# Reordering the start of a fused attention and FFN kernel: the last v tile's copy, the kv matmuls and the small copies of the prologue

## The chip, the cores and the metric

The kernel runs on one core of a Trainium2 chip. The metric is device time in microseconds (us), the median of several executions; lower is better. The kernel before takes 211.5 us, and its executions spread over 0.4 us in the first rounds.

The engines are named as in the profile: PE (TensorE), PEld (its weight loads), DVE (VectorE), ACT (ScalarE), POOL (GpSimd) and SP (SyncE, which issues most of the DMA transfers here). "Line L262" is a line of the kernel's source.

## The reference, cut to what matters

```python
batch, n_heads, seq, head_dim, r = 4, 4, 1088, 32, 8
def phi(x):                                   # S1, S2 are [8, 32]
    a = einsum('rd,bhsd->bhsr', S1, x)
    b = einsum('rd,bhsd->bhsr', S2, x)
    return outer(a, b) flattened to 64 features
q_p, k_p = phi(q), phi(k)
kv  = einsum('bhsf,bhsd->bhfd', k_p, v)       # sum over the sequence
z   = sum of k_p over the sequence
out = (q_p @ kv) / (q_p . z + 1e-6)           # num / den
x   = out as [4352, 128]
return square(relu(x @ w_in)) @ w_out         # w_in [128, 2048], w_out [2048, 128]
```

The attention of a batch needs all of its k and v before its first output. So the first batch has a prologue, in which TensorE waits for other engines again and again. After it, the FFN of one chunk of rows runs beside the attention of the next.

## The kernel before: the parts that matter

The transfers of the first batch, in order. SyncE issues them, except part 2 of v (the last v tile), which ScalarE issues. A transfer is said here to land when the last of its 16 semaphore increments shows in the trace:

```python
load_qk(kn[0], k, 0, 0, 512)
load_qk(kn[0], k, 0, 512, S)
load_qk(qn[0], q, 0, 0, 384)          # first 384 columns of q
load_v(vn[0], 0, 0)
load_v(vn[0], 0, 2, (nc.scalar, nc.scalar))   # the last v tile, issued by ScalarE
load_v(vn[0], 0, 1)
# ... w_in: two transfers of 512 KB
load_qk(qn[0], q, 0, 384, S)          # the other columns of q
# ... w_o: two transfers of 512 KB
```

GpSimd's small copies, which stand ahead of its copy of the last v tile:

```python
for h in range(H):
    for j_, o_, f_ in (...three patterns...):
        nc.gpsimd.tensor_copy(_ap(sr, ...), _ap(s_T, ...))     # 12 copies
for h in range(H):
    nc.gpsimd.tensor_copy(sq[...], s_T[:, 0:16])               # 4 copies
iden = cpool.tile([128, 128], F32); make_identity(nc, iden[:])
iden16 = ...; nc.gpsimd.tensor_copy(iden16[:], iden[:])
```

And the order of the prologue, which is each engine's order too, since the schedule is by hand:

```python
keep_warm(WARM0)                      # 11 matmuls on zeros
# ... kf (features of k), fs (their copy), four groups of tiles: 2, 2, 4, 1
replicated(2, 0, 128, psf, "pg")
a_v(0, 0, nc.scalar); a_kp(0, 0); a_kv0(0); a_kp(0, 1)
a_kv(0, 0); a_kv(0, 1)                # kvp += v_t^T kp_t
replicated(0, 0, 128, psa, "feat"); replicated(1, 0, 128, psa, "tr")
a_fs(0, 2); a_fs(0, 3)
a_v(0, 1, nc.scalar)
a_v(0, 2, nc.gpsimd)                  # the last v tile, 64 rows
a_kp(0, 2); a_kp(0, 3)
for t in range(2, 9): a_kv(0, t)
nc.scalar.copy(qb[:, 0:128], rep[2, 0][:, 0:128]); products(0, 128)
# ... replicated(j, 128, 384) for j = 2, 0, 1
nc.scalar.copy(qb[:, 128:384], rep[2, 128][:, 0:256])
a_kvz(0)                              # kvp transposed and copied: 8 small copies
products(128, 384)
# ... w_in cast to 16 bits on ScalarE
for t in range(3): a_nd(0, t)         # numerators and denominators
a_qT(0, 384, S)                       # VectorE transposes the other columns of q
a_qc(0, 1); a_qc(0, 2, psf, "po")     # TensorE, from that transpose
keep_warm(WARM)                       # 4 more matmuls on zeros
a_x1(0, 0); a_x2(0, 0)                # den, rden, mx, ... on VectorE
a_x3(...); a_xp(...); a_xT(...)       # xs, its transpose xp, the FFN's input xT
```

The names: kvp is the sum of v times features of k, and kvz its transposed copy; rep is S applied to q, from which `products` forms q's features qp; nd holds numerators and denominators; qc is S applied to the other columns of q, for later chunks; pg is the first product of the FFN. The warm matmuls compute nothing: they hold TensorE's clock up.

## Time and profile before

| | before |
|---|---|
| median | 211.5 us (211.44 to 211.83, 4 runs) |
| profiled execution | span 209.2 us |
| last v tile copied | 11.37 to 11.65 us |
| last kvp matmul ends | 12.12 us |
| nd ends | 15.28 us |
| den starts | 15.32 us |
| first FFN matmul, pg | 18.15 us |

The table by windows shows where TensorE is full (columns: window, its length, busy time and instructions of PE, PEld, DVE, ACT, POOL, then TensorE's clock, DMA share, GB/s).

```profile
10.00:15.00 5.00, 4.12 (x58) 3.39 (x54) 2.96 (x10) 2.14 (x5) 1.77 (x8) 1.00 1.04 341
...
25.00:40.00 15.00, 15.00 (x97) 9.16 (x97) 12.02 (x35) 12.92 (x28) 6.15 (x32) 1.00 0.03 10
```

From 25 us on PE is busy all of the time. Nothing that the change does touches that part, so its worth is how much earlier the FFN starts.

The chain of waits of the first 21 us, in order of time (start, duration, what):

```profile
...
6.87 1.59 POOL sr L228 x3
8.51 1.13 POOL sq L233
...
11.42 0.24 POOL va_119 L253
...
11.70 0.42 PE kvp L321 x8
12.12 1.49 PE rep L598 x6
...
13.69 1.60 PE nd L382 x12
```

GpSimd works through sr, sq and the identity and only then copies the last v tile. The last eight kvp passes wait for that copy, and rep and nd follow on TensorE with hardly a gap.

The timeline of the same stretch (start, duration, engine, line, operation; in brackets the idle time before and what ended it):

```profile
11.37 0.28 POOL L253 COPY va_119<-vn 64x128 f32<-64x128 f32 x1
11.70 0.42 PE L321 MATMUL kvp<-kp,va_119 128*33 128x64 f32 x8 [0.80 <-POOL va_119 L253]
13.69 1.59 PE L382 MATMUL nd<-kvz_125,qp 128*128 128x132 f32 x12
14.07 0.90 DVE L259 STREAM_TRANSPOSE qT<-qn 128x704 f32<-128x704 f32 x1
15.32 0.17 DVE L398 TENSOR_SCALAR den<-nd 128x12 f32<-128x12 f32 x1 [0.34 <-PE nd L382]
18.15 0.22 PE L477 MATMUL pg<-xT,w_in 128*128 128x128 f16 x1
```

The transpose of q's other columns starts at 14.07 us, and the semaphore events of the trace show the transfer that it reads (qn, columns 384 on) landing at 14.01 us.

### The profile page before, as it was taken

The page shows a single profiled execution, that of the slowest core. Times are in us where ns is not written, and L with a number is a line of the kernel's source. Part 1 is how long each engine was busy: PE and PEld are TensorE (multiplying, and loading weights), DVE is VectorE, ACT ScalarE, POOL GpSimd, SP SyncE. Part 2 cuts the span into 40 slices and gives each one's busy share as a digit, 9 for nine tenths or more (in the row PEclk, how much of TensorE's full clock was granted, in tenths as well). Part 3 has the DMA queues.
Part 4 walks back from the last instruction along what each step waited for, and adds up shares of the span by engine and source line. Part 5 has one row for each costly group of instructions (what it writes and reads, how often), then busy time and mean ns, then how long its engine had stood idle before and what let it go on. Part 6 is the DMA issues. An engine that isn't in the chain of part 4 may idle for free.

```text
span 209.2 us, 3744 instructions
## 1 busy us (share of the span) xinstructions
PE 200.6 (96%) x1213; PEld 125.3 (60%) x1213; DVE 146.5 (70%) x393; ACT 145.1 (69%) x327; POOL 61.9 (30%) x254
## 2 busy tenths in 40 slices
PE   7988999999999999999999999999999999999980
PEld 2864675566677655567676655557766655555650
DVE  3856967948597697795577877695487776667740
ACT  2555988747898876487888776487887775756740
POOL 4924556010076840010573700010573500000001
PEclk9999999999999999999999999999999999999998
DMA  6599400200047220020006710020002010110201
GB/s 186 144 342 245 132 0 3 36 5 0 0 75 190 96 33 0 3 39 0 2 12 165 185 31 0 3 39 3 0 6 33 0 31 3 19 19 0 38 0 32
DMA packets 26728, 11.24 MB, mean 54 GB/s; under 512 B 18822, under 2 KB 25286, under 8 KB 26710
## 3 DMA queue, kind: packets, MB, share of 16 engines
q1 hardware_dynamic: 26244, 10.89, 21.4%
q8 instruction: 9, 0.15, 0.3%
q10 hardware_dynamic: 386, 0.07, 0.2%
q0 software_dynamic: 80, 0.07, 0.1%
q14 instruction: 9, 0.07, 0.1%
HBM read 8.78 MB, written 2.23 MB: 53 GB/s over the span
## 4 chain that ended last, share of the span: by engine, by line
PE 68%; issue 20%; POOL 5%; DVE 3%; DMA 1%; POOLq 0%; ACT 0%; ACTq 0%; DVEq 0%
PE po L499 39%; PE pg L477 11%; PE nd L382 8%; PE kvp L321 4%; PE qc L356 3%; POOL br L515 2%; PE kf L275 2%; POOL sr L228 1%; DMA s_nat<-in_S_dram 1%; PE xp L455 1%; POOL sq L233 1%; PE rep L598 1%; DVE xs L439 1%; DVE mx L403 0%; POOLq L786 0%
## 5 line engine op out<-in xcount | busy, mean ns | idle before, releaser
L486 ACT ACTIVATE gt<-pg 128x384 f32<-128x384 f32 (+2 forms) x193 | 89.5, 465 | 42.6 <-PE pg L477 41.0
L477 PE MATMUL pg<-xT,w_in 128*128 128x384 f16 (+2 forms) x193 | 61.1, 317 | 0.5 <-ACT xT L464 0.3
L515 POOL COPY br<-beta 32x3 f32<-32x3 f32 x192 | 44.3, 231 | 55.7 <-DVE beta L446 48.3
L477 PEld LDWEIGHTS <-w_in 128*128 128x128 f16 x193 | 18.8, 98 | 18.9 <-issue 1.7
L568 POOL DMA_DIRECT2D out_dram<-obl x1 | 0.8, 813 | 38.6 <-DVE obl L559 38.6
L366 DVE STREAM_SHUFFLE qa<-qc 128x384 f32<-128x384 f32 x22 | 11.9, 592 | 0.0
L382 PEld LDWEIGHTS nd<-kvz_127,qp 128*128 128x128 f32 x72 | 10.0, 190 | 2.5
L382 PEld LDWEIGHTS nd<-kvz_125,qp 128*128 128x128 f32 x72 | 9.7, 190 | 2.9 <-issue 0.4
L301 DVE TENSOR_TENSOR kp<-fs 128x1024 f32<-128x1024 f32 (+3 forms) x10 | 11.0, 1110 | 0.5 <-ACT fs L289 0.2
L371 DVE TENSOR_TENSOR qp<-qa,qb 128x384 f32<-128x384 f32 x22 | 11.2, 548 | 0.1
L382 PE MATMUL nd<-kvz_127,qp 128*128 128x132 f32 x72 | 10.1, 276 | 0.0
L382 PE MATMUL nd<-kvz_125,qp 128*128 128x132 f32 x72 | 10.0, 277 | 0.1
L398 DVE TENSOR_SCALAR den<-nd 128x12 f32<-128x12 f32 x12 | 2.0, 171 | 11.3 <-PE nd L382 11.3
L523 DVE STREAM_TRANSPOSE oT<-po 128x384 f32<-128x384 f32 (+1 forms) x11 | 6.2, 564 | 5.4 <-PE po L499 5.2
L342 POOL COPY kvz_127<-kvt 32x2 f32<-32x2 f32 x8 | 1.5, 185 | 28.3 <-DVE kvt L332 28.0
L356 PE MATMUL qc<-qT,sq 128*128 128x384 f32 x22 | 9.0, 496 | 0.0
L464 ACT COPY xT<-xp 128x384 f16<-128x384 f16 (+3 forms) x13 | 5.6, 428 | 2.3 <-PE xp L455 2.2
L581 PE MATMUL warm<-zero 128*128 128x512 f16 x15 | 5.8, 557 | 1.2 <-DVE zero L142 1.2
L439 DVE TENSOR_TENSOR xs<-nd,sc 128x384 f16<-128x384 f32 (+2 forms) x13 | 6.7, 520 | 0.2
L321 PEld LDWEIGHTS kvp<-kp,va_122 128*33 128x33 f32 x144 | 4.3, 111 | 3.8 <-issue 3.8
L361 DVE STREAM_SHUFFLE qb<-qc 128x384 f32<-128x384 f32 x11 | 6.5, 590 | 0.0
L321 PEld LDWEIGHTS kvp<-kp,va_119 128*33 128x33 f32 x144 | 4.3, 111 | 3.4 <-issue 2.2
(677 smaller groups left out, 431.1 us busy)
## 6 DMA issues: line engine op xcount, KB each, us to landing
vn<-in_v_dram SPq DMA_DIRECT2D x32, 64.0 KB, 3.7
kn<-in_k_dram SPq DMA_DIRECT2D x3, 544.0 KB, 4.8
qn<-in_q_dram SPq DMA_DIRECT2D x3, 544.0 KB, 3.4
out_dram<-ob SPq DMA_DIRECT2D x32, 48.0 KB, 1.8
w_in_99<-in_moe_w_in_dram SPq DMA_DIRECT2D x2, 512.0 KB, 4.7
w_o<-in_moe_w_out_dram SPq DMA_DIRECT2D x2, 512.0 KB, 9.4
out_dram<-ob SPq DMA_DIRECT2D x12, 40.0 KB, 1.7
qn<-in_q_dram SPq DMA_DIRECT2D x1, 352.0 KB
```

What stands on the lines that cost most here:

```text
L301: nc.vector.tensor_tensor(out=_ap(kp, 0, 128, 0, [[64, 4 * n], [8, 8], [1, 8]]), in0=_ap(fs, 0, 128, 0, [[8, 4 * n], [1, 8], [0, 8]]), in1 ...
L321: nc.tensor.matmul(kvp[c : c + 33, 64 * (h // 2) : 64 * (h // 2) + 64], va[b % 2][:, 132 * t + 33 * h : 132 * t + 33 * h + 33], kp[:, c0 + ...
L356: nc.tensor.matmul(qc[:, 0:384], sq[:, :], qT[:, 384 * ch : 384 * ch + 384])
L361: nc.vector.stream_shuffle(in_=st[b, "qc", ch][:, 0:384], out=qb[:, :], mask=mask_b)
L366: nc.vector.stream_shuffle(in_=st[b, "qc", ch][:, 0:384], out=qa[:, :], mask=mask_a[e])
L371: nc.vector.tensor_tensor(out=qp[:, :], in0=st[b, "qa", ch, e][:, :], in1=st[b, "qb", ch][:, :], op=mult)
L382: nc.tensor.matmul(nd[:, 132 * o : 132 * o + 132], st[b, "qp", ch, e][:, 128 * o : 128 * o + 128], st[b, "kvz"][:, 132 * e : 132 * e + 132 ...
L439: nc.vector.tensor_tensor(out=_ap(st[b, "xs", ch], 0, 128, 128 * o, [[32, 4 * n], [1, 32]]), in0=_ap(st[b, "nd", ch], 0, 128, 132 * o, [[3 ...
L477: nc.tensor.matmul(pg[:, c0:c1], w_in[:, 128 * c : 128 * c + 128], st[b, "xT"][:, 384 * ch + c0 : 384 * ch + c1],)
L486: nc.scalar.activation(gt[:, c0:c1], pg[:, c0:c1], Relu)
L499: nc.tensor.matmul(st["po", b, ch][:, c0:c1], w_o[:, 128 * c : 128 * c + 128], g2s[i][1][:, c0:c1], start=(c == 0 and c0 == 0), stop=(c == ...
L515: nc.gpsimd.tensor_copy(_ap(st[b, "br"], 32 * dm, 32, 12 * ch + p0, [[4, 3]]), st[b, "beta"][32 * p0 : 32 * p0 + 32, 3 * ch : 3 * ch + 3],)
```

## The change

The intent is to end the kvp sums sooner. The last v tile is copied ahead of sq and the identity; four of the twelve sr copies go to ScalarE; four kv tiles instead of two run ahead of the replicated features; kp is grouped 2, 2, 2, 3; the v copy is split; the eight kvz copies, already shared by VectorE, ScalarE and GpSimd, are shared out differently and stand ahead of the second qb copy; and there are two warm matmuls less. (A short description that came with it says that ScalarE copies the last v tile. The diff leaves that copy on GpSimd, earlier in its order.)

```diff
-    WARM0, WARM = 11, 4
+    WARM0, WARM = 10, 3
-    KG = [[(0, 2), (2, 2), (4, 4), (8, 1)]] + ...
+    KG = [[(0, 2), (2, 2), (4, 2), (6, 3)]] + ...
+    a_kv0(0)                       # moved up from behind a_kp(0, 0)
-    for h in range(H):
-        for j_, o_, f_ in (... three patterns, all nc.gpsimd ...):
+    for j_, o_, f_, copy in (
+        (2, ..., nc.gpsimd.tensor_copy),
+        (1, ..., nc.scalar.copy),
+        (0, ..., nc.gpsimd.tensor_copy),
+    ):
+        for h in range(H):
-    # sq copies and the identity stood here
     (in a_kvz)
-            block(nc.vector, h)
+            block(nc.vector if b > 0 or h < 2 else nc.scalar, h)
-            ones(nc.gpsimd if b > 0 or h < 2 else nc.scalar, h)
+            ones(nc.gpsimd if b > 0 or h > 1 else nc.vector, h)
     (in the prologue)
-    a_kv(0, 0)
-    a_kv(0, 1)
+    for t in range(4):
+        a_kv(0, t)
-    a_v(0, 1, nc.scalar)
     a_v(0, 2, nc.gpsimd)
+    # sq copies and the identity, now here
+    a_v(0, 1, nc.scalar, 0, 2)
     a_kp(0, 2)
+    a_v(0, 1, nc.scalar, 2, 2)
     a_kp(0, 3)
-    for t in range(2, 9):
+    for t in range(4, 9):
+    a_kvz(0)
     nc.scalar.copy(qb[:, 128:384], rep[2, 128][:, 0:256])
-    a_kvz(0)
```

More of the change, by code (lines that the diff above doesn't have):

```diff
@@ L79 @@
     E = 2
-    WARM0, WARM = 11, 4
+    WARM0, WARM = 10, 3
     LA = 3
-    KG = [[(0, 2), (2, 2), (4, 4), (8, 1)]] + [[(0, 4), (4, 5)]] * (B - 1)
+    KG = [[(0, 2), (2, 2), (4, 2), (6, 3)]] + [[(0, 4), (4, 5)]] * (B - 1)
     add = mybir.AluOpType.add
@@ L197, with a_kv0 @@
     st = {}
+    def a_kv0(b):
+        st[b, "kvp"] = psa.tile([128, 512], F32, tag="acc", bufs=2, name="kvp")
+        nc.vector.memset(st[b, "kvp"][:, 0:128], 0.0)
+    a_kv0(0)
     def a_kT(b, part):
@@ L225 @@
         )
-    for h in range(H):
-        for j_, o_, f_ in ((2, 8, [[0, 4], [1, 8]]), (0, 0, [[1, 4], [0, 8]]), (1, 4, [[1, 4], [0, 8]])):
-            nc.gpsimd.tensor_copy(
+    for j_, o_, f_, copy in (
+        (2, 8, [[0, 4], [1, 8]], nc.gpsimd.tensor_copy),
+        (1, 4, [[1, 4], [0, 8]], nc.scalar.copy),
+        (0, 0, [[1, 4], [0, 8]], nc.gpsimd.tensor_copy),
+    ):
+        for h in range(H):
+            copy(
                 _ap(sr, 32 * h, 32, 128 * j_ + 32 * h, [[8, 4], [1, 8]]),
@@ L231, with a_v @@
             )
-    for h in range(H):
-        nc.gpsimd.tensor_copy(
-            sq[32 * h : 32 * h + 32, 32 * h : 32 * h + 16], s_T[:, 0:16]
-        )
-    iden = cpool.tile([128, 128], F32)
-    make_identity(nc, iden[:])
-    iden16 = cpool.tile([128, 128], F16)
-    nc.gpsimd.tensor_copy(iden16[:], iden[:])
     mask_b = [8 + l % 8 for l in range(32)]
     mask_a = [[4 * e + l // 8 for l in range(32)] for e in range(E)]
-    def a_v(b, part, eng):
+    def a_v(b, part, eng, t0=0, n=4):
         a = va[b % 2]
@@ L248, in a_v @@
             copy(
-                _ap(a, 0, 128, 528 * part, [[33, H], [132, 4], [1, 32]]),
-                _ap(vn[b], 0, 128, 512 * part, [[128, H], [32, 4], [1, 32]]),
+                _ap(a, 0, 128, 528 * part + 132 * t0, [[33, H], [132, n], [1, 32]]),
+                _ap(vn[b], 0, 128, 512 * part + 32 * t0, [[128, H], [32, n], [1, 32]]),
             )
@@ L308, in a_kp @@
             st[b, "kp", t0 + i] = kp, 256 * i
-    def a_kv0(b):
-        st[b, "kvp"] = psa.tile([128, 512], F32, tag="acc", bufs=2, name="kvp")
-        nc.vector.memset(st[b, "kvp"][:, 0:128], 0.0)
     def a_kv(b, t):
@@ L614 @@
     a_kp(0, 0)
-    a_kv0(0)
     a_kp(0, 1)
-    a_kv(0, 0)
-    a_kv(0, 1)
+    for t in range(4):
+        a_kv(0, t)
     replicated(0, 0, 128, psa, "feat")
@@ L622 @@
     a_fs(0, 3)
-    a_v(0, 1, nc.scalar)
     a_v(0, 2, nc.gpsimd)
+    for h in range(H):
+        nc.gpsimd.tensor_copy(
+            sq[32 * h : 32 * h + 32, 32 * h : 32 * h + 16], s_T[:, 0:16]
+        )
+    iden = cpool.tile([128, 128], F32)
+    make_identity(nc, iden[:])
+    iden16 = cpool.tile([128, 128], F16)
+    nc.gpsimd.tensor_copy(iden16[:], iden[:])
+    a_v(0, 1, nc.scalar, 0, 2)
     a_kp(0, 2)
+    a_v(0, 1, nc.scalar, 2, 2)
     a_kp(0, 3)
-    for t in range(2, 9):
+    for t in range(4, 9):
         a_kv(0, t)
```

## The prediction

> **What bounds it now.** From about 20 us on, TensorE is the limit: the table by windows shows it 100% busy in every window from 25 to 200 us, and the chain of waits is almost only its matmuls. The change touches only the first 19 us; after them the order of instructions on each engine is the same. So the gain is how much earlier the first FFN matmul (pg, 18.15 us in the timeline) starts.
>
> Up to 15.3 us the chain of waits runs over GpSimd: twelve sr copies (5.24 to 8.46), four sq copies (to 10.44), the identity (to 11.4), the copy of the last v tile (to 11.66). Then come kvp's last 8 passes (11.70), rep 128:384 (12.12 to 13.61), nd (13.69 to 15.29), the DVE chain den to xs (15.32 to 17.85), xp, xT, pg.
>
> **What the change does.** (The short description says ScalarE copies the last v tile. The diff leaves it on GpSimd, ahead of sq and the identity.)
> - GpSimd: four of twelve sr copies (0.27 us each) go to ScalarE, which idles 3.07 us there. The last v tile is copied at about 7.4 instead of 11.4 us.
> - TensorE: one warm matmul less (0.43 us) lets kf start about 0.4 us earlier.
> - kp regrouped 2,2,2,3, the kvp memset (0.17 us) moved to idle time. ScalarE's first v copy stays at 7.38 because its DMA lands at 7.32, the second at 8.95 because its DMA lands at 8.85. The last kp still ends near 9.9.
> - So kvp ends at about 10.7 instead of 12.12: 1.4 us won. rep follows to about 12.2. kvz copies (0.2 us each) are shared and done before that. nd then ends at about 13.75 instead of 15.29.
>
> **Why most of it will not arrive.** den stands on VectorE behind the transpose of qT 384:1088 (0.90 us). The Trainium skill ("TensorE: Matmul & The Clock Gate", opening table) says VectorE's queue is strict FIFO. That transpose needs the qn transfer of columns 384 on, whose semaphore increments in the trace end at 14.01 us; the transpose started at 14.07. The transfers are issued by SyncE in the same order with the same waits, and none waits for compute, so that landing stays. Before, the landing and the end of the products (14.16) coincided, and it cost nothing. After, VectorE idles from about 12.8 to 14.05, transposes until 14.95, and den starts at about 14.98 instead of 15.32. Gain: 0.35 of the 1.5 us. qc also waits for this transpose, as before (15.03); three warm matmuls instead of four clear TensorE by about 17.2, when the first xs is ready.
>
> Other transfers do not bind: w_in lands at 11.7 and 13.0, w_o's first half at 16.8 (needed at 19.1).
>
> **Predicted:** 211.5 - 0.35 = 211.15 us, range 210.3 to 211.6. The chance of over 2% faster is 0.01, within 2% 0.985, slower by over 2% 0.005.
>
> **What the profile would show.** kvp's last matmuls end at 10.4 to 11.0 with no wait for GpSimd; nd ends by 14.0; VectorE's longest prologue wait is now qT <- DMA qn, 1 us or more, at about 14.0; den starts at 14.8 to 15.1 right behind qT, with no wait for nd; pg starts at about 17.8; the windows after 25 us are unchanged but shifted.
>
> **What would make it wrong.** If the qn transfer lands earlier in undisturbed runs than in this trace, up to 1.5 us shows (210.0). If it lands later, or TensorE's 1.3 us gap before qc lowers its clock, nothing or a small loss shows. If ScalarE's four sr copies are slower than 0.25 us and delay the first fs copy past 6.4, the kp chain slips, but 1.2 us of slack now covers that.

## The result, and the profile after

Ratios here and below are the mean time of one kernel's runs over that of the other's runs of the same rounds, so they are not quite the ratio of the medians.

| | before | after |
|---|---|---|
| median | 211.5 us | 210.64 us (210.21 to 211.34, 4 runs) |
| ratio | | 0.9959 (95%: 0.993 to 0.9988) |
| span of the profiled execution | 209.2 us | 208.4 us |
| last v tile copied | 11.37 to 11.65 | 8.58 to 9.48 |
| last kvp matmul ends | 12.12 | 10.73 |
| nd ends | 15.28 | 13.86 |
| qn (columns 384 on) lands | 14.01 | 13.61 |
| den starts | 15.32 | 14.47 |
| pg starts | 18.15 | 17.43 |

The kernel became 0.4% faster. The timeline after, the lines that answer to those of before:

```profile
8.58 0.90 POOL L256 COPY va_119<-vn 64x128 f32<-64x128 f32 x1
9.41 1.31 PE L319 MATMUL kvp<-kp,va_119 128*33 128x64 f32 x40
12.10 1.76 PE L380 MATMUL nd<-kvz_125,qp 128*128 128x132 f32 x12
13.63 0.91 DVE L262 STREAM_TRANSPOSE qT<-qn 128x704 f32<-128x704 f32 x1 [0.77 <-DMA qn<-in_q_dram]
14.47 0.13 DVE L396 TENSOR_SCALAR den<-nd 128x12 f32<-128x12 f32 x1
14.60 1.56 PE L354 MATMUL qc<-qT,sq 128*128 128x384 f32 x4 [0.74 <-DVE den L396]
17.43 0.90 PE L475 MATMUL pg<-xT,w_in 128*128 128x128 f16 x3
```

TensorE no longer waits for GpSimd in kvp, and nd ends 1.42 us sooner. But the transpose is now preceded by a wait of 0.77 us for the transfer, and den comes straight behind the transpose with no wait for nd in its brackets: only 0.85 us of the 1.42 reach den. The rest waits for q. qc, on TensorE, is put down to den, but the instruction that it needs is the transpose; the two end within 0.06 us of each other.

The chain of waits after, over the same 21 us, has no GpSimd in it any more:

```profile
2.14 3.91 DMA vn<-in_v_dram
...
7.86 5.75 DMA qn<-in_q_dram
...
13.63 0.91 DVE qT L262
14.54 0.07 DVE den L396
14.61 1.55 PE qc L354 x4
16.16 0.66 PE warm L579 x3
...
16.86 0.23 PE xp L453
```

The chain goes from the transfers of the first microseconds through SyncE's issues to the qn transfer, the transpose, qc, the warm matmuls and xp. So two paths lead from the transpose to the FFN: den to xs on VectorE, and qc and the warm matmuls on TensorE. The second is the longer one here by a little: xp's first weights (xs) are loaded at 16.67 us, but the warm matmuls hold TensorE until 16.82. Of den's 0.85 us, 0.72 reach pg. The full part is unchanged; the window from 25 to 40 us after:

```profile
25.00:40.00 15.00, 15.00 (x96) 8.76 (x96) 12.04 (x32) 13.00 (x29) 6.15 (x32) 1.00 0.06 15
```

### The profile page after: what moved, and what is told of

The parts are those of the page before. It is cut to its first block, busy times and chain, and to the rows that moved or that the text cites. A ratio compares the mean times of both kernels' runs of the same rounds, so it can differ in the third digit from the quotient of the medians.

```text
span 208.4 us, 3741 instructions
## 1 busy us (share of the span) xinstructions
PE 200.1 (96%) x1211; PEld 124.9 (60%) x1211; DVE 146.4 (70%) x393; ACT 146.2 (70%) x332; POOL 61.2 (29%) x250
## 4 chain that ended last, share of the span: by engine, by line
PE 68%; issue 19%; DMA 5%; POOL 2%; DVE 2%; SPq 1%; ACT 0%; POOLq 0%
PE po L497 39%; PE pg L475 11%; PE nd L380 7%; PE qc L354 4%; PE kvp L319 4%; DMA qn<-in_q_dram 3%; POOL br L513 2%; DMA vn<-in_v_dram 2%; PE kf L278 2%; PE xp L453 1%; SPq L103 1%; DVE qT L262 0%; SPq L158 0%; POOLq L792 0%; SPq L113 0%
## 5 line engine op out<-in xcount | busy, mean ns | idle before, releaser
L304 DVE TENSOR_TENSOR kp<-fs 128x512 f32<-128x512 f32 (+3 forms) x10 | 10.9, 1111 | 0.2
L319 PEld LDWEIGHTS kvp<-kp,va_122 128*33 128x33 f32 x144 | 4.3, 111 | 3.8 <-issue 3.8
L579 PE MATMUL warm<-zero 128*128 128x512 f16 x13 | 5.1, 557 | 1.2 <-DVE zero L142 1.2
L401 DVE TENSOR_REDUCE mx<-nd 128x12 f32<-128x384 f32 x12 | 5.9, 495 | 0.0
```

The lines of the kernel that those rows point to most:

```text
L304: nc.vector.tensor_tensor(out=_ap(kp, 0, 128, 0, [[64, 4 * n], [8, 8], [1, 8]]), in0=_ap(fs, 0, 128, 0, [[8, 4 * n], [1, 8], [0, 8]]), in1 ...
L319: nc.tensor.matmul(kvp[c : c + 33, 64 * (h // 2) : 64 * (h // 2) + 64], va[b % 2][:, 132 * t + 33 * h : 132 * t + 33 * h + 33], kp[:, c0 + ...
```

## The experiments

Theory A: after the change, the start of the FFN is set by the landing of the qn transfer, since den stands behind the transpose of q in VectorE's order. Rivals: the gain comes from kf starting 0.5 us sooner (one warm matmul less) and the shared copies, with nothing waiting for the transfer; or the change itself moved the landing.

All times that follow in one table; "before" was run in the same rounds.

| run | median us | before us | ratio (95%) |
|---|---|---|---|
| after_again | 210.80 | 211.40 | 0.9973 (0.9955 to 0.9990) |
| after_qn_early | 210.47 | 211.40 | 0.9961 (0.9942 to 0.9980) |
| before_qn_early | 211.20 | 211.40 | 0.9999 (0.9975 to 1.0024) |
| before_v_early | 210.92 | 211.40 | 0.9981 (0.9963 to 0.9999) |
| after_v_late | 211.39 | 211.48 | 0.9990 (0.9969 to 1.0010) |
| after_qn_late | 217.76 | 211.48 | 1.0303 (1.0266 to 1.0339) |
| after_warm | 210.83 | 211.48 | 0.9976 (0.9952 to 0.9999) |
| after_third | 210.54 | 211.37 | 0.9956 (0.9922 to 0.9990) |
| qn_early_qb_first | 210.12 | 211.37 | 0.9930 (0.9900 to 0.9960) |
| qn_mid_qb_first | 210.04 | 211.37 | 0.9922 (0.9890 to 0.9955) |
| after_qT_late | 211.88 | 211.37 | 1.0007 (0.9970 to 1.0045) |
| qn_mid_again | 210.57 | 211.80 | 0.9954 (0.9902 to 1.0006) |

### The changed kernel again: after_again and after_third

No edit.

> The changed kernel, unedited, once more, for a second look at the landing of the qn transfer (columns 384 on). Theory A (the start of den is set by that landing plus 0.05 us and the 0.91 us transpose): den starts 0.9 to 1.0 us after the landing again; if it lands at 14.0 as in the trace of before, den starts near 14.9 and the span is about 0.4 us longer than in the first trace of the changed kernel, if at 13.6 it repeats that trace. Theory B (the change itself moves the landing): the landing is 13.6 again and later in every run of the kernel before. Time: ratio 0.996 to 0.998.

> The changed kernel unedited, as the measure for the three runs beside it. By both earlier looks: ratio 0.996 to 0.998, den at 14.4 to 14.9, 0.9 us behind the landing of the qn transfer.

Measured: the ratio came out at 0.9973 and 0.9956, so with the first look (0.9959) the gain is 0.6 to 0.9 us. The qn transfer landed at 13.56 and 13.80, and den started at 14.41 and 14.66, each time 0.85 to 0.86 us behind the landing, as in the first trace. That the distance stays while the landing moves is what theory A asks for.

About theory B, the landing: in six traces with the changed kernel's transfers it was 13.56 to 13.94 us, in the two traces of kernels that keep the order of before (before and before_v_early) 14.01 and 14.54. The run before_qn_early speaks against the change as a cause: SyncE's first eleven transfers there are those of the kernel before, and so is all work beside them, yet the twelfth was issued at 6.83 us, as in the changed kernel (6.91) and not as in the trace of before (7.37). And two variants of the changed kernel with the same first eleven transfers (qn_early_qb_first and qn_mid_qb_first, below) issued the twelfth at 7.33 and 7.38, as late as before. So the landings that SyncE waits for vary by half a microsecond with the same program. With two traces against six, whether the kernel before lands later on average stays open. The gain does not hang on it, since den of the kernel before waits for nd and not for this transfer.

### The transfer earlier, on both kernels: after_qn_early and before_qn_early

```diff
+    load_qk(qn[0], q, 0, 384, S)
     w_in32 = cpool.tile([128, DFF], F32)
     ... (w_in's two transfers)
-    load_qk(qn[0], q, 0, 384, S)
```

> The changed kernel with the qn transfer issued before the two w_in transfers. Theory A: it lands at 11.5 or sooner, VectorE's wait for it is gone, the transpose runs at about 12.9, den starts right behind nd at 13.9 instead of 14.5, the time falls by another 0.5 to 1.0 us, to about 209.8 us. Rival (the landing is no bound; the gain comes from the earlier kf and nothing is left to win): within 0.2 us of the changed kernel.

> The kernel before with the qn transfer issued before the two w_in transfers. Theory A: nd ends at 15.29 for reasons on GpSimd, so den stays at 15.3 and the time within 0.2 us of before. Rival (the late transfer bound both kernels alike): 0.5 us or more faster.

In both the transfer landed near 10 us (9.90 and 10.01). First the changed kernel with it, then the kernel before with it, from the timeline:

```profile
12.31 1.79 PE L380 MATMUL nd<-kvz,qp 128*128 128x132 f32 x12
13.02 0.90 DVE L262 STREAM_TRANSPOSE qT<-qn 128x704 f32<-128x704 f32 x1
14.14 0.17 DVE L396 TENSOR_SCALAR den<-nd 128x12 f32<-128x12 f32 x1 [0.22 <-PE nd L380]
16.97 0.22 PE L475 MATMUL pg<-xT,w_in 128*128 128x128 f16 x1
```

```profile
15.26 0.17 DVE L398 TENSOR_SCALAR den<-nd 128x12 f32<-128x12 f32 x1 [0.34 <-PE nd L382]
18.09 0.22 PE L477 MATMUL pg<-xT,w_in 128*128 128x128 f16 x1
```

The kernel before gains nothing (0.9999): its den waits for nd and starts where it did. In the changed kernel the wait for the transfer is gone, den waits for nd again, and pg starts 0.41 us sooner than in after_again (17.38). The gain is smaller than the 0.5 to 1.0 us expected, because nd is right behind: it ended at 14.10 instead of 13.87, since the v transfers issued just ahead of qn landed at 9.10 instead of 8.40 us and the v copy with them. In the time, 210.47 against 210.80, the difference of 0.3 us lies between the rival's 0.2 and theory A's 0.5 us, and the two intervals overlap. So one run shows what binds (the first wait moves from the DMA to nd), and the size of what is left, a few tenths, is near the noise.

### The transfer later: after_qn_late

```diff
-    load_qk(qn[0], q, 0, 384, S)
     ... (w_o's two transfers)
+    load_qk(qn[0], q, 0, 384, S)
```

> The changed kernel with the qn transfer issued behind w_o. Theory A: the transfer lands about 3 us later (w_o moves 1 MB at some 340 GB/s), near 16.5, the transpose and den follow it, pg too, and the time grows by 2.5 to 3.5 us over the changed kernel. Rival (the landing is no bound): under 0.5 us.

```profile
18.91 0.91 DVE L262 STREAM_TRANSPOSE qT<-qn 128x704 f32<-128x704 f32 x1 [5.65 <-DMA qn<-in_q_dram]
19.75 0.13 DVE L396 TENSOR_SCALAR den<-nd 128x12 f32<-128x12 f32 x1
```

The transpose started 5.28 us later than in the changed kernel, den the same 5.28 us. That is what theory A forecast: nd had ended at 14.26, and only the two w_o transfers traded places with this one. The rival's 0.5 us is out. The size was missed: 217.76 is 6.93 us over after_warm, the changed kernel but for two warm matmuls in the same rounds, where 2.5 to 3.5 were expected. The transfer landed at 18.89, later than the estimate from 340 GB/s: fifteen of its sixteen increments had come by 17.37, the last one 1.5 us after them. And there was a second cost, seen in the table by windows:

```profile
15.00:20.00 5.00, 0.12 (x1) 0.12 (x1) 1.05 (x3) 0.00 (x0) 0.00 (x0) 0.64 1.02 282
20.00:25.00 5.00, 4.61 (x13) 2.06 (x14) 2.69 (x13) 0.88 (x4) 2.19 (x12) 0.68 0.43 113
```

TensorE idled for 5.6 us, and its clock stood at 0.50 of full from 16.41 to 23.24 us (the 0.64 and 0.68 of these lines are means over 5 us at 1.00 and at 0.50), where the changed kernel has 1.00. The four qc matmuls took 2.93 us instead of 1.56. The Trainium skill ("TensorE: Matmul & The Clock Gate", "Why this matters for your kernels") warns of idle gaps of more than about 3 us, after which the clock halves; this trace agrees on the halving, though it came 2.15 us after nd's last matmul ended. The changed kernel's gap before qc, 0.74 us, left the clock at 1.00. From den to pg it took 4.61 us here (19.75 to 24.36) and 2.96 in the changed kernel. pg is 6.93 us later than in the changed kernel: 5.28 are the transfer, and the other 1.65 lie in this stretch of slower matmuls.

### Only the place in VectorE's order: after_qT_late

```diff
-    WARM0, WARM = 10, 3
+    WARM0, WARM = 10, 7
-    a_qT(0, 384, S)
-    a_qc(0, 1)
-    a_qc(0, 2, psf, "po")
     ... (a_x1 to a_xT)
-    a_qb(0, 1)
+    a_qT(0, 384, S)
     ... (the first FFN matmuls)
+    a_qc(0, 1)
+    a_qb(0, 1)
     ... (the first ffn2)
+    a_qc(0, 2, psf, "po")
```

> The changed kernel with the transfers as they are, but the transpose of qT 384 on moved behind den to xs on VectorE, and its two qc matmuls behind the first FFN matmuls (7 warm matmuls fill TensorE's wait). It tells whether den's wait is only its place in VectorE's queue. Theory A: den starts at 13.9, right behind nd, with the qn transfer landing as late as ever; pg starts near 16.9. But the qc matmuls (1.5 us), which stood in TensorE's idle time, now stand in its busy time, so the total is between 0.3 us faster and 1 us slower than the changed kernel. Rival (den needs that transfer or transpose by data): den stays at 14.4 or later.

```profile
12.96 1.79 PE L380 MATMUL nd<-kvz,qp 128*128 128x132 f32 x12
14.79 0.17 DVE L396 TENSOR_SCALAR den<-nd 128x12 f32<-128x12 f32 x1 [1.03 <-PE nd L380]
17.30 0.91 DVE L262 STREAM_TRANSPOSE qT<-qn 128x704 f32<-128x704 f32 x1
19.02 0.81 PE L354 MATMUL qc<-qT,sq 128*128 128x384 f32 x2
```

den now runs 2.5 us ahead of the transpose, right at the end of nd, so it needs neither the transfer nor the transpose by data: what made it wait was the order alone. The Trainium skill's opening table ("TensorE: Matmul & The Clock Gate") calls the queue of VectorE strict FIFO, and this pair of traces agrees. In this execution nd itself ended late, at 14.75 against 13.86 (kf's matmuls ended at 8.44, not 7.55: the clock of TensorE reached 1.00 only at 7.25 us, against 5.13 in the trace of the changed kernel and 4.1 to 6.4 in the other twelve), so den's start is no sooner than in the changed kernel and the expected 13.9 was not met. The time is worse than the changed kernel's in the same rounds, 211.88 against 210.54, 0.34 us more than the 1 us allowed for. It fits that qc, which stood in TensorE's idle time, now runs at 19.02 and 20.32 in its busy time. Hiding the wait this way costs more than it wins.

### One part alone: before_v_early

The kernel before, with only GpSimd's order changed.

```diff
-    for h in range(H):
-        nc.gpsimd.tensor_copy(sq[...], s_T[:, 0:16])
-    ... (identity)
     a_v(0, 1, nc.scalar)
     a_v(0, 2, nc.gpsimd)
+    for h in range(H):
+        nc.gpsimd.tensor_copy(sq[...], s_T[:, 0:16])
+    ... (identity)
```

> The kernel before with only GpSimd's order changed: the last v tile copied right after the twelve sr copies, ahead of sq and the identity. Theory A: the copy starts near 8.5 instead of 11.4, kvp ends at 10.8 to 11.0 instead of 12.12, nd near 14.2, den waits for the qn transfer's transpose: the whole gain of the change, 0.4 to 0.9 us, without its other parts. Rival (the gain comes from kf starting 0.5 us earlier, one warm matmul less, and from sharing copies with ScalarE): at most 0.3 us.

```profile
8.65 1.24 POOL L245 COPY va<-vn 64x128 f32<-64x128 f32 x1
9.98 1.76 PE L313 MATMUL kvp<-kp,va 128*33 128x64 f32 x56
...
14.57 0.91 DVE L251 STREAM_TRANSPOSE qT<-qn 128x704 f32<-128x704 f32 x1 [0.79 <-DMA qn<-in_q_dram]
15.40 0.13 DVE L390 TENSOR_SCALAR den<-nd 128x12 f32<-128x12 f32 x1
```

One move already brings the kernel to the wall of the transfer: VectorE waits 0.79 us for it, and den follows the transpose. The ratio is 0.9981, a gain of 0.4 us (interval 0.02 to 0.8), against 0.9973 of the whole change in the same rounds; the intervals overlap, and the rival's 0.3 us is not excluded by the times. The traced execution was this kernel's slowest (211.31, the others 210.68 to 211.13), with a landing at 14.54, and its pg started at 18.58, no sooner than in the trace of before; so the trace shows the wall, and only the times show the gain. kvp ended at 11.74, later than the 10.8 to 11.0 expected: the passes of seven tiles, 1.76 us, stand behind the second v copy here, where the whole change has five (1.31 us), and they began at 9.98 instead of 9.41, since TensorE's first rep matmuls had waited 0.82 us for the sr copies, all twelve of them on GpSimd here. Those are the parts of the kv reordering and of the sr copies on ScalarE, and they were hidden behind the transfer in this trace.

### That part undone: after_v_late

```diff
-    a_v(0, 2, nc.gpsimd)
     ... (sq, identity)
     nc.gpsimd.tensor_copy(iden16[:], iden[:])
+    a_v(0, 2, nc.gpsimd)
```

> The changed kernel with the last v tile copied behind sq and the identity again, all else as changed. Theory A: GpSimd has four sr copies less, so the copy comes at about 10.4 instead of 8.6, kvp ends at about 11.2 instead of 10.65, nd near 14.4, still ahead of or level with the end of the qT transpose (14.5): within 0.2 us of the changed kernel. Rival (the place of that copy is what pays): 0.5 us or more slower than the changed kernel.

```profile
10.95 0.29 POOL L256 COPY va<-vn 64x128 f32<-64x128 f32 x1
11.29 0.42 PE L319 MATMUL kvp<-kp,va 128*33 128x64 f32 x8 [0.76 <-POOL va L256]
```

Here the copy started at 10.95, kvp waited 0.76 us for it and ended at 11.71, nd at 14.84; the transpose ended at 14.88 and den started there. The two limits met, so theory A's mechanism is seen again, but the copy came 0.5 us later than expected. The ratio, 0.9990, lies nearer to before than to the changed kernel. The expectation of "within 0.2 us" was not met: 211.39 is 0.56 us over after_warm, the nearest kernel in the same rounds, and pg started at 17.76 against 17.43 after the change. The intervals overlap, but by both numbers the place of the copy pays, and the rival named in that expectation was nearer than theory A's estimate.

### The warm matmuls put back: after_warm

```diff
-    WARM0, WARM = 10, 3
+    WARM0, WARM = 11, 4
```

> The changed kernel with the kernel before's warm matmuls, 11 and 4 instead of 10 and 3. Theory A: kf starts 0.4 us later, which the slack before the qn landing covers; the fourth warm matmul before xp holds TensorE 0.2 us longer, since there qc and the warm matmuls end just as xs is ready: 0.1 to 0.3 us slower than the changed kernel. Rival (the gain is the earlier kf): 0.4 us or more slower.

0.9976, about as for the changed kernel (0.9956 to 0.9973), so the warm matmuls are not the gain. In the trace kf started at 5.37 us with eleven of them, hardly later than with ten (5.33): the expected 0.4 us did not appear, so this trace does not test a late kf. The kept traces show why. What the eleventh matmul costs depends on when TensorE's clock reaches 1.00. Where it did so after 5.7 us, kf started at 5.83 and 5.90 with eleven (before, before_qn_early) and at 5.47 with ten (after_qn_late, after_qT_late); here it did so at 4.83, the matmuls sped up, and kf came 0.1 us behind the sk copies that it needs. The qn transfer landed at 13.62, den started at 14.48, and pg at 17.66, 0.23 us later than after the change, as the fourth warm matmul before xp would do it.

### Toward a faster version: qn_early_qb_first, qn_mid_qb_first, qn_mid_again

```diff
     for c in range(2):
         ... (w_in's transfer c)
+        if c == 0: load_qk(qn[0], q, 0, 384, S)     # "mid"; "early" is ahead of the loop
-    load_qk(qn[0], q, 0, 384, S)
-    a_kvz(0)
     nc.scalar.copy(qb[:, 128:384], rep[2, 128][:, 0:256])
+    a_kvz(0)
```

> The changed kernel with the qn transfer ahead of w_in, and ScalarE's qb copy ahead of its two kvz blocks again. With the qn transfer early alone, nd became the limit: it ended at 14.10, since its second and third tiles wait for products(128, 384), those for qb, and qb stood behind ScalarE's kvz blocks. Theory A: qb comes 0.4 us sooner, the products 0.2 to 0.3 us sooner, nd ends near 13.8, den right behind it: 0.4 to 0.8 us faster than the changed kernel. Rival (qb's place costs nothing, kvz's readiness starts nd): as with the early transfer alone, 0.25 us faster than the changed kernel.

> The same with the qn transfer between the two w_in transfers. With it ahead of both, the second v part landed 0.5 us later (9.10 against 8.60 and 8.40). Theory A with that contention: here qn lands near 12.3, early enough for VectorE at 12.7, and v is as in the changed kernel, so kvp ends near 10.7, nd near 13.6: 0.6 to 0.9 us faster than the changed kernel. Rival (the later landing of v was chance): no better than the run with the transfer ahead of both.

> The kernel with the qn transfer between the two w_in transfers and qb first, unedited, once more, since its profiled execution was one of its slow ones (210.53, against 209.68 to 209.89 in three others) and showed the qn transfer landing at 14.02, not near 12.3 as expected. If the early place helps by an earlier landing, a trace of a quick execution (209.9 or less) has the landing before 13.0 and den right behind nd; if a quick execution has it at 13.6 or later too, the gain over the changed kernel comes from something else. Time: ratio 0.990 to 0.995 again if the version is really faster than the changed kernel (0.9956 to 0.9973 in three looks).

The idea of qb first failed in the traces. With it nd started at 12.59 to 12.81 instead of 12.10, since ScalarE's kvz copies came later, and in every case nd ended 3.2 us after kvp did, against 3.1 us in the changed kernel. Here is the second trace of the "mid" version:

```profile
12.72 1.59 PE L381 MATMUL nd<-kvz,qp 128*128 128x132 f32 x12 [0.17 <-DVE qp L603]
13.17 0.91 DVE L263 STREAM_TRANSPOSE qT<-qn 128x704 f32<-128x704 f32 x1
14.34 0.17 DVE L397 TENSOR_SCALAR den<-nd 128x12 f32<-128x12 f32 x1 [0.27 <-PE nd L381]
17.17 0.22 PE L476 MATMUL pg<-xT,w_in 128*128 128x128 f16 x1
```

In it the qn transfer landed at 13.14, ahead of the end of nd, and den waited for nd. That execution took 210.36 us. In the first trace of the same kernel the transfer landed at 14.02 and the execution took 210.53, so the place between the two w_in transfers doesn't hold the landing: there the first w_in transfer landed at 13.10 instead of 11.3, and q with it. The expected 12.3 was met in neither, nor did either trace fall on an execution under 209.9.

Are these versions faster than the changed kernel? In the rounds that they shared with after_third they had 0.9930 and 0.9922 against 0.9956, medians 0.42 and 0.50 us lower; but the intervals overlap, and the repeat of one gave 0.9954. The four runs with an earlier transfer have ratios of 0.9922 to 0.9961, the three of the changed kernel 0.9956 to 0.9973. The traces say that den no longer waits for the transfer when it lands early, which is worth at most the few tenths until nd binds. I take them as probably 0.3 us faster, and not as settled. The version with the transfer ahead of w_in and nothing else is the simplest of them.

### Why the copy was late at all: small copies on GpSimd

This had no run of its own; it is read from both traces. The groups by shape (line, engine, operation, count, busy us, mean ns). First the kernel before from 5.2 to 6.7 us, then from 6.6 to 9.7 us; VectorE forms kp in most of the second window.

```profile
L228 POOL COPY sr<-s_T 32x32 f32<-32x32 f32 x9 | 1.5, 201 | 0.1
```

```profile
L228 POOL COPY sr<-s_T 32x32 f32<-32x32 f32 x5 | 1.9, 421 | 0.0
L233 POOL COPY sq<-s_T 32x16 f32<-32x16 f32 x2 | 1.4, 712 | 0.1
L301 DVE TENSOR_TENSOR kp<-fs 128x1024 f32<-128x1024 f32 x1 | 1.2, 1224 | 0.1
```

And the changed kernel from 6.6 to 9.7 us:

```profile
L239 POOL COPY sr<-s_T 32x32 f32<-32x32 f32 x3 | 1.9, 619 | 0.1
L256 POOL COPY va_119<-vn 64x128 f32<-64x128 f32 x1 | 0.9, 901 | 0.1
```

The sr copy takes 0.2 us alone and 0.4 to 0.6 on average while VectorE multiplies fs with fs; the first sq copy took 1.13, the last 0.19. The last v tile takes 0.90 us there and 0.28 in the kernel before, where VectorE stood idle beside it. The Trainium skill ("GPSIMD Engine Reference", "1. Specifications") says that GpSimd shares its SBUF interfaces with VectorE and that instructions of VectorE with two SBUF inputs contend; kp is such an instruction, and these traces agree. The kept traces go further. In after_v_late the same copy, moved to where VectorE stands idle, took 0.29 us instead of 0.90. In all eight traces in which the v copy began during a kp instruction, it ended 0.15 us after that instruction (kp at 9.33 and the copy at 9.48 in the changed kernel, 9.74 and 9.89 in before_v_early). In the two in which it began up to 0.03 us ahead of kp (after_third, after_qT_late), it took 0.28 us, and kp took 0.82 and 0.80 instead of 0.69. In a third, qn_mid_qb_first, kp began only 0.10 us before the copy's end, and neither was slowed. So whichever began second was held up by the other. That the shared interface is the reason is the page's.

## Why the prediction was right, and where its size was off

It was right in time (210.64 in a range of 210.3 to 211.6) and in mechanism, and low in size: 0.35 us of gain predicted, 0.6 to 0.9 measured in three looks. Each of the three intervals by itself still contains 0.35 us (a ratio of 0.9983); it is the traces that show which term was off.

- *kvp to end near 10.7, nd near 13.75, with no wait for GpSimd.* Measured 10.73 and 13.86. Right, though two terms in it were off: the sr copies ended at 8.52 instead of 7.4 (they met VectorE's kp), and the last kp at 9.33 instead of 9.9. Neither mattered, since kvp's last forty passes started at 9.41, when ScalarE's second v copy ended.
- *Most of the 1.5 us will not arrive, since den stands behind the transpose that waits for the transfer.* Right: shown in the trace after, where the wait for the transfer appears and den has none of its own; by the later transfer, which moved den by the same 5.28 us; and by after_qT_late, where den ran ahead of the transpose.
- *The landing stays at 14.01.* This is the mis-sized term. It landed at 13.61 in the trace after, and at 13.56 and 13.80 in the two further looks. den followed it, 0.85 us behind. The prediction's 14.98 for den is 0.51 later than the 14.47 measured: 0.40 of that is the landing, and the rest is that den was recorded 0.86 us after the landing, not 0.97. The prediction knew that an earlier landing would show as more gain, but put the number of one trace where a spread of 0.4 us and more belonged. An estimate: with 13.72, the mean of the six landings of the changed kernel's order, the same sum puts den 0.86 us later, at 14.58, a gain of 0.74 us at den, less about 0.1 for the warm matmuls; that is inside the 0.6 to 0.9 measured.
- *VectorE's wait of 1 us or more for the transfer.* 0.77 us, for the same reason.
- *ScalarE's v copy stays at 7.38 because its transfer lands at 7.32.* It started at 6.88. Again an arrival read from one trace and taken as fixed.
- *One warm matmul less lets kf start 0.4 us earlier.* kf started at 5.33 instead of 5.83, but at 5.37 with the warm matmul put back. The 0.4 us appears only in traces in which the clock comes up late, and putting the matmuls back had no clear effect on the time.
- *Three warm matmuls clear TensorE when xs is ready.* Nearly: xs was ready for xp at 16.67, the warm matmuls end at 16.82 and xp starts at 16.86; with four, pg was 0.23 us later.
- *The windows after 25 us unchanged.* Right; PE is busy in all of 25 to 40 us in both.

## What to carry to other kernels

Before shortening a chain, look for what else would be due at about the same moment: here a transfer landed 1.3 us before the end of the chain, at no cost, and took 40% of the gain as soon as the chain was shorter. Instructions that are independent by data still wait for each other in the order of an engine, so put what waits for a late transfer behind what is urgent, or bring the transfer forward, and check what either does to the engine that fills its idle time. A landing time read from one trace is a sample: take two or three traces before a prediction depends on a few tenths of it.

## What the Trainium skill lacked or had wrong

- No page that I read tells how much the landing of the same transfer varies between executions. Here one transfer of 352 KB, issued behind 1 MB of w_in, landed at 13.56 to 13.94 us in six traces and at 14.01 and 14.54 in two others, with the same transfers in the same order ahead of it in all eight. Its issue lay at 7.57 to 8.42 us, and from issue to landing it took 5.7 to 6.2 us.
- "TensorE: Matmul & The Clock Gate", "Why this matters for your kernels": its bound of about 3 us on idle gaps is too wide for after_qn_late. There the clock went to 0.50 at 16.41 us, 2.15 us after the last matmul ended (14.26), in a gap of 5.6 us, and it came back to 1.00 at 23.24, 3.36 us after the matmuls had begun again (19.88). The changed kernel's gap of 0.74 us before qc left it at 1.00.
